# Attention decode on one core: all V tiles in one buffer, the last tiles in pieces, K and V loads in turn, PSUM zeroed by ScalarE and VectorE

## The chip, the cores and the metric

The kernel runs on one core of one Trainium2 chip. A core has a matrix engine (TensorE, PE in the profile), a vector engine (VectorE, DVE), a scalar engine (ScalarE, ACT), GpSimd (POOL), and SyncE (SP), which here does nothing but issue DMAs. Sixteen DMA engines bring data from HBM into SBUF; matrix products land in PSUM. The metric is device microseconds of one execution, lower is better: the median of three runs of the kernel before is 655.73 us (655.61 to 658.28).

## What is computed

One decode step of grouped-query attention. One query token with 32 heads reads a cache of 65,536 keys and values for 8 key/value heads; four query heads share one key/value head. Everything is bf16, the head size is 128.

```python
def reference(q, k, v):          # q: 1 x 32 x 1 x 128, k and v: 1 x 8 x 65536 x 128
    ...
    k = jnp.repeat(k, rep, axis=1)
    v = jnp.repeat(v, rep, axis=1)
    scale = D ** -0.5
    scores = jnp.einsum("bhqd,bhkd->bhqk", q, k) * scale
    p = _softmax(scores, axis=-1)
    return jnp.einsum("bhqk,bhkd->bhqd", p, v)
```

K and V together are 268.4 MB, and each byte is used once.

## The kernel before

**Tiles.** For each of the 8 key/value heads (g = 0 to 7) K and V are cut in two halves of 32,768 keys (b = 0, 1). One such half is a tile: 128 partitions, 256 keys in each, 64 KB in each partition, 8.39 MB in all. There are 32 tiles. They are named here K00, K01 (head 0), K10, K11, up to K71, and V00 to V71. The buffer `io` has room for three tiles: slot 0 for V, slot 1 for K of half 0, slot 2 for K of half 1.

**What happens to a K tile.** VectorE transposes it in place in four instructions of 64 keys a partition (L227). Each of them releases two groups of eight matmuls (L370), which add the scores of the tile to the PSUM tensor `sc`. A tile has eight groups; each group counts up `s_sc` by one. `sc` is four PSUM banks; half b fills banks 2b and 2b+1. The matmuls only ever add (`start=False`), so something must set `sc` to zero before a head begins.

**Softmax of a head.** When both K tiles of a head are scored, VectorE takes the maximum of each bank (L232), then of all (L237); TensorE turns it (L412), VectorE takes the maximum for each query head (L241 to L249), ScalarE computes the exponentials of the four banks and their sums (L252) and then counts up `s_ls`, and VectorE transposes the exponentials into `et`, half a head at a time (L263, `weights`).

**What happens to a V tile.** 64 matmuls (L339) multiply `et` by the tile and add to the PSUM tensor `vacc`, which also must be zero at the start of a head. At the end of a tile `s_vc` goes up by one. After both V tiles of a head VectorE folds `vacc` into `vs` (L272, L275, `collect`), TensorE gathers it (L335), VectorE scales it (L287), and a small DMA writes the head's output.

**TensorE's order.** Its program is one loop over h = 0 to 8. At its head it gathers the output of head h-2 (waits for `s_vs`), sums the exponentials (L352, waits for `s_ls`), and writes zeros with five matmuls of a zero matrix into `sc` and `vacc` (L356). Then, for j = 0 and 1: the scores of K tile (h, j), and then the V tile that is two half-steps behind, which is V(h-1, j). So V tiles are always multiplied behind the scores of the next head's K tile.

**VectorE's order.** For each g: the transposes of K(g,0); the wait for V(g-1,0) to be multiplied; `weights(g-1, 1)`; the transposes of K(g,1) with the bank maxima among them; the fold of `vacc`; the softmax of g; `weights(g, 0)`.

**SyncE's order** is the order of the loads, and a load whose wait is not over holds back all behind it. It is K00, K01, V00, K10, K11, V01 and from then on K and V in turn (K20, V10, K21, V11, ...). K(g,b) waits until the scores of K(g-1,b) are done, and V tile number n waits until all n tiles before it are multiplied (`s_vc`). The end is different: V70 goes into slot 1 in two halves as soon as the scores of K70 are done, and V71 into slot 0, in six pieces of 128, 64, 32, 16, 8 and 8 keys (`CUTS`), once V61 is multiplied.

**The last head's V.** V70 lies in slot 1, and so has code of its own in TensorE's loop: 16 turns of a loop of four matmuls (L390), each of which writes the same 16 PSUM rows; GpSimd passes on the landing of its two halves (`s_un`), and each turn counts up `s_vu`. VectorE's `weights(7, 1)` waits for all 16 turns. V71 is multiplied by L339, except its last 16 keys, which go straight into the output product (L423, `TAIL`).

Of the kernel before, what the change touches and what calls it, by code (L numbers as in the profile page):

```python
# [9 lines left out]
ACT = mybir.ActivationFunctionType  # L10
# [3 lines left out]
P = 128  # L14
D = 128
SL = 256
# [3 lines left out]
WB = 160  # L20
PS = 64
TAIL = 16
UN = 16
CUTS = [0, 128, 192, 224, 240, 248, 256]


# [22 lines left out]
def kernel(  # L49
# [15 lines left out]
    def sb(name, shape, dt):  # L65
        return ctx.enter_context(nc.sbuf_tensor(name, shape, dt))
# [7 lines left out]

    io = sb("io", [P, 3 * SL, D], bf16)
    wz = sb("wz", [P, 4, WB], bf16)
    zero = sb("zero", [P, 512], bf16)
# [24 lines left out]
    pf = ps("pf", [P, 512])  # L102
    pl, fin = pb[0:H, 8:12], pf[0:H, 0:D]

    s_q, s_ka, s_kb, s_st = sem("s_q"), sem("s_ka"), sem("s_kb"), sem("s_st")
    s_v = [sem(f"s_v{i}") for i in range(len(CUTS) - 1)]
    s_u = [sem(f"s_u{i}") for i in range(2)]
    s_un = sem("s_un")
# [6 lines left out]
    s_sc, s_pe, s_vb, s_vc, s_vu = sem("s_sc"), sem("s_pe"), sem("s_vb"), sem("s_vc"), sem("s_vu")  # L115

    sp, act, dve, gp, pe = nc.sync, nc.scalar, nc.vector, nc.gpsimd, nc.tensor
    SP = Queue(nc, sp, None)
# [8 lines left out]
    def load(src, g, b, at, s, lo=0, hi=SL):  # L127
        sp.dma_start(
            out=io[:, at * SL + lo:at * SL + hi, :], in_=rows(src, g, b)[:, lo:hi, :]
        ).then_inc(s, 16)  # L130

    def load_k(g, b):
# [36 lines left out]
    GP.mark(gp.memset(zero[:, :], 0.0))  # L169
    n = GP.mark(gp.memset(ident[:, :], 0.0))  # L170
    GP.after(n)
    p_ident = GP.mark(gp.affine_select(
# [1 line left out]
        pattern=[[-1, P]], channel_multiplier=1,  # L174
    ))
    DV.mark(dve.memset(one[:, :], 1.0))
    dve.memset(ls[:, :], 0.0).then_inc(s_ls, 1)
    dve.memset(vs[:, :], 0.0).then_inc(s_vs, 2)
    DV.wait((s_gp, p_ident))

    DV.mark(dve.tensor_reduce(
# [33 lines left out]
            ).then_inc(s_w, 1)  # L215
    GP.wait((s_sc, 16 * G))
    gp.sem_inc(s_w, 4)
    for i in range(2):
        GP.wait((s_u[i], 16))
        gp.sem_inc(s_un, 128 // UN)  # L220


    def transposes(g, b):
        DV.wait(((s_ka, s_kb)[b], 16 * (g + 1)))
        for t0 in range(0, SL, PS):
            part = io[:, (1 + b) * SL + t0:(1 + b) * SL + t0 + PS, :].rearrange("p t d -> p (t d)")
            dve.transpose(out=part.bitcast(u32), in_=part.bitcast(u32)).then_inc(s_kt, 2)  # L227
            yield
# [10 lines left out]
    def softmax(g):  # L239
        DV.wait((s_pe, 4 * g + 3))  # L240
        n = DV.mark(dve.tensor_reduce(  # L241
            out=m4[:, :], in_=pt[0:1, 0:P].rearrange("o (x h) -> o h x", h=H), axis=AX.X, op=ALU.max
        ))
        DV.after(n)
        dve.tensor_scalar_mul(
            out=nrow[:, :, :], in0=m4[:, None, :].to_broadcast([1, 32, H]), scalar1=-SCALE
        ).then_inc(s_nr, 1)
        DV.wait((s_pe, 4 * g + 4))
        d_nmb = DV.mark(dve.tensor_copy(out=nmb[:, :], in_=pb[:, 0:1]))  # L249
        ACTQ.wait((s_dv, d_nmb))  # L250
        for b in range(4):
            a = act.activation(  # L252
                out=ex[:, b, :], in_=sc[:, 512 * b:512 * b + 512], func=ACT.Exp, bias=nmb[:, :],
                scale=SCALE, accum_out=ls[:, b:b + 1],
            )
            ACTQ.mark(a)
        act.wait_ge(s_ac, ACTQ.n)
        act.sem_inc(s_ls, 1)

    def weights(g, b):  # L260
        for i in range(2):
            DV.wait((s_ac, 4 * g + 2 * b + i + 1))
            dve.transpose(out=et[:, i, :], in_=ex[:, 2 * b + i, :]).then_inc(s_et, 1)  # L263

    def reciprocal(g):
# [2 lines left out]
        DV.after(n)  # L268
        return DV.mark(dve.reciprocal(out=rl[:, :], in_=l4[:, :]))

    def collect():
        n = DV.mark(dve.tensor_scalar_mul(out=vs[:, :], in0=vacc[:, 0, :], scalar1=sely[:, 0:1]))  # L272
        for y in range(1, 4):
            DV.after(n)
            i = dve.scalar_tensor_tensor(  # L275
                out=vs[:, :], in0=vacc[:, y, :], scalar=sely[:, y:y + 1], in1=vs[:, :],
                op0=ALU.mult, op1=ALU.add,
            )
            if y < 3:
                n = DV.mark(i)  # L280
            else:
                i.then_inc(s_vs, 1)

    def finish(g, n_pe, d_rl):
        DV.wait((s_st, 16 * g), (s_pe, n_pe))
# [6 lines left out]
    for g in range(G):  # L292
        for _ in transposes(g, 0):
            pass
        if g:
            DV.wait((s_vc, 2 * g - 1))
# [7 lines left out]
        top()  # L304
        if g:
            d_rl = reciprocal(g - 1)
            DV.wait((s_vc, 2 * g))
            collect()
        softmax(g)
        weights(g, 0)  # L310
        if g:
            finish(g - 1, 4 * g + 5, d_rl)
    DV.wait((s_vu, SL // UN))
    weights(G - 1, 1)
    d_rl = reciprocal(G - 1)
    DV.wait((s_vb, 2 * G - 1))
    collect()
    finish(G - 1, 4 * G + 3, d_rl)
    SP.wait((s_st, 16 * G))

# [25 lines left out]
    with nc.Fori(0, G + 1, 1, engines=OrderedEngineSet([PE]), head_slot={PE: 0}) as h:  # L346
# [3 lines left out]
        gather(start=True, stop=True).then_inc(s_pe, 1)  # L350
        take(s_ls, 1)
        pe.matmul(out=pl, lhsT=sel[:, :], rhs=ls[:, :], start=True, stop=True).then_inc(s_pe, 1)  # L352
        for bank in [sc[:, 512 * b:512 * b + 512] for b in range(4)] + [
            vacc[:, :, :].rearrange("p y d -> p (y d)")
        ]:
            pe.matmul(  # L356
                out=bank, lhsT=zero[:, 0:P], rhs=zero[:, :], start=True, stop=False,
                skip_group_check=True,
            )
        with pe.Fori(0, 2) as j:  # L360
            with pe.If(h < G):
                with pe.Fori(0, 8) as n:
# [18 lines left out]
                    i.then_inc(s_sc, 1)  # L381
            with pe.If(h * 2 + j > 1):
                take(s_et, 2)
                with pe.If(h * 2 + j == 2 * G):
                    with pe.Fori(0, SL // UN) as n:
                        r_v = n * (UN * D) + SL * D
                        r_e = (n // 8) * 512 + (n // 4) % 2 * 16 + (n % 4) * 128
                        take(s_un, 1)
                        for c in range(4):
                            i = pe.matmul(  # L390
                                out=vacc[0:16, :, :],
                                lhsT=bass.AP(et, r_e + c * 32, [[1024, P], [1, 16]]),
                                rhs=bass.AP(io, r_v + c * (4 * D), [[IO, P], [1, 4 * D]]),
                                start=False, stop=False, skip_group_check=True,
                            )
                        i.then_inc(s_vu, 1)
                with pe.Else():
                    for ch in range(4):
                        if ch != 1:
                            take(s_v[max(ch - 1, 0)], 16)  # L400
                        for tt in range(16 if ch < 3 else 12):
                            if (ch, tt) == (3, 8):
                                take(s_v[3], 16)
                            i = wide(ch, tt)
                    i.then_inc(s_vb, 1)
                    with pe.If(h < G):
                        for tt in range(12, 16):
                            i = wide(3, tt)
# [50 lines left out]
```

## Time and profile before

| | |
|---|---|
| median of the runs | 655.73 us |
| the profiled execution, its own time | 658.72 us |
| its span, first to last instruction | 655.3 us |
| PE busy, PE weight loads | 376.2 us, 147.6 us |
| DVE busy | 342.4 us |
| ACT busy, POOL busy | 23.6 us, 7.9 us |
| TensorE clock granted, mean | 0.831 |
| read from HBM | 268.44 MB |

No compute engine is busy for more than 57% of the span. The profile has a row of the rate of the DMAs in 40 slices, a list of DMA issues with the time from issue to landing, and a timeline, whose columns are the start, the duration, engine, line, operation and tensors, the count of merged instructions, and in brackets the idle time before the first of them with what ended it. Where VectorE's transposes (L227) are ended by a DMA, their start tells when a K tile has landed.

### The profile page before, as it was taken

What the parts mean: (1) busy time and instruction counts of PE and PEld (TensorE: products, weight loads), DVE (VectorE), ACT (ScalarE), POOL (GpSimd) and SP (SyncE); (2) the same over time, 40 slices, a digit from 0 to 9 for tenths busy, and PEclk for the clock granted to TensorE, in tenths of its full rate; (3) what the DMA queues carried; (4) which work ended last, traced back from release to release, by engine and by line L of the source; (5) the groups of instructions that cost most, each with busy time, mean ns of one, the idle gap of its engine ahead of it and who ended that gap; (6) DMA issues with size and microseconds to landing.
All of it is one profiled execution on the core that took longest, in us unless ns stands there. A gap on an engine that the chain in (4) does not pass through costs nothing. (4 is left out here: it accounts for less than half of the span.)

```text
span 655.3 us, 7257 instructions
## 1 busy us (share of the span) xinstructions
PE 376.2 (57%) x2167; PEld 147.6 (23%) x2167; DVE 342.4 (52%) x226; ACT 23.6 (4%) x65; POOL 7.9 (1%) x40
## 2 busy tenths in 40 slices
PE   1187466764818656284744838266580866628655
PEld 0032122221303222031311313122130322203212
DVE  1588192936439292564808466193733829156201
ACT  0000100010000100001000010001000010000100
POOL 1000000000000000000000000000000000000000
PEclk9999769795978879597895959879596886959898
DMA  9999991999999999999999999999999999999970
GB/s 382 448 448 400 436 444 68 448 448 413 420 448 444 440 396 448 444 444 392 448 448 444 424 412 448 444 444 392 445 448 444 416 420 448 448 436 396 443 330 0
DMA packets 5589, 268.50 MB, mean 410 GB/s; under 512 B 720, under 2 KB 720, under 8 KB 1104
## 3 DMA queue, kind: packets, MB, share of 16 engines
q1 hardware_dynamic: 5480, 268.44, 94.9%
q10 hardware_dynamic: 104, 0.02, 0.0%
q14 instruction: 4, 0.03, 0.0%
q8 instruction: 1, 0.02, 0.0%
HBM read 268.44 MB, written 0.01 MB: 410 GB/s over the span
## 5 line engine op out<-in xcount | busy, mean ns | idle before, releaser
L370 PE MATMUL sc<-io,wz 128*128 x1024 | 272.5, 418 | 217.0 <-PEq L325 174.6
L227 DVE STREAM_TRANSPOSE io<-io 128x4096 uint32<-128x4096 uint32 x64 | 279.5, 4415 | 109.4 <-DMA io<-in_k_dram 109.4
L370 PEld LDWEIGHTS sc<-io,wz 128*128 x1024 | 106.0, 104 | 386.8 <-issue 308.6
L263 DVE STREAM_TRANSPOSE et<-ex 128x512 bf16<-128x512 bf16 x32 | 21.5, 701 | 117.3 <-PE vacc L339 81.3
L339 PE MATMUL vacc<-io,et 128*16 128x512 bf16 x956 | 55.7, 387 | 5.3 <-PEq L325 5.3
L232 DVE TENSOR_REDUCE mx<-sc 128x1 f32<-128x512 f32 x32 | 20.8, 668 | 49.7 <-PE sc L370 49.7
L252 ACT ACTIVATE ex<-sc,nmb 128x512 bf16<-128x512 f32 x32 | 21.6, 685 | 589.8 <-DVE nmb L249 589.8
L339 PEld LDWEIGHTS vacc<-io,et 128*16 128x16 bf16 x956 | 24.6, 91 | 36.3 <-issue 14.1
L390 PE MATMUL vacc<-io,et 128*16 x64 | 16.7, 384 | 9.6 <-PEq L325 9.6
L356 PE MATMUL sc<-zero 128*128 128x512 bf16 x36 | 17.0, 628 | 0.0
L272 DVE TENSOR_SCALAR vs<-vacc,sely 128x128 f32<-128x128 f32 x8 | 2.8, 350 | 24.6 <-PE vacc L339 24.6
L352 PE MATMUL pb<-ls,sel 128*4 128x4 f32 x18 | 1.8, 169 | 19.1 <-PEq L325 19.1
L212 POOL COPY wz<-qT 32x16 bf16<-32x16 bf16 x32 | 6.1, 191 | 520.0 <-PE sc L370 516.7
L414 PE MATMUL pb<-one,nrow 1*128 1x1 f32 x16 | 2.8, 241 | 14.3 <-PEq L325 14.3
L390 PEld LDWEIGHTS vacc<-io,et 128*16 x64 | 5.5, 86 | 21.2 <-issue 17.9
L335 PE MATMUL pf<-vs,sel 128*4 128x128 f32 x20 | 4.2, 295 | 9.9 <-PEq L325 9.2
L275 DVE SCALAR_TENSOR_TENSOR vs<-vacc,sely,vs 128x128 f32<-128x128 f32 x24 | 8.4, 351 | 0.9
L252 ACT ACTIVATION_READ_ACCUMULATOR ex<-sc,nmb 128x1 f32 x32 | 6.5, 202 | 0.0
L352 PEld LDWEIGHTS pb<-ls,sel 128*4 128x4 f32 x18 | 1.2, 86 | 21.6 <-issue 21.4
L414 PEld LDWEIGHTS pb<-one,nrow 1*128 1x128 f32 x16 | 2.3, 182 | 15.6 <-issue 15.6
L356 PE MATMUL vacc<-zero 128*128 128x512 bf16 x9 | 5.7, 634 | 0.0
L356 PEld LDWEIGHTS sc<-zero 128*128 128x128 bf16 x36 | 3.9, 131 | 5.3 <-issue 5.0
(29 smaller groups left out, 23.9 us busy)
## 6 DMA issues: line engine op xcount, KB each, us to landing
io<-in_v_dram SPq DMA_DIRECT2D x3, 4096.0 KB, 38.0
io<-in_v_dram SPq DMA_DIRECT2D x1, 2048.0 KB, 23.6
io<-in_v_dram SPq DMA_DIRECT2D x1, 1024.0 KB, 25.7
io<-in_v_dram SPq DMA_DIRECT2D x1, 512.0 KB, 26.4
io<-in_v_dram SPq DMA_DIRECT2D x2, 256.0 KB, 26.7
io<-in_k_dram SPq DMA_DIRECT2D x16, 47.7
io<-in_v_dram SPq DMA_DIRECT2D x14, 28.9
out_dram<-o ACTq DMA_DIRECT2D x7, 1.0 KB
```

The costliest lines, as they stand in the source:

```text
L212: gp.tensor_copy(out=wz[r, :, c0:c0 + H].rearrange("p (s w) h -> p s w h", s=2), in_=qTb[r, :, :, g, :],).then_inc(s_w, 1)
L227: dve.transpose(out=part.bitcast(u32), in_=part.bitcast(u32)).then_inc(s_kt, 2)
L232: return DV.mark(dve.tensor_reduce(out=mx[:, b:b + 1], in_=sc[:, 512 * b:512 * b + 512], axis=AX.X, op=ALU.max))
L252: a = act.activation(out=ex[:, b, :], in_=sc[:, 512 * b:512 * b + 512], func=ACT.Exp, bias=nmb[:, :], scale=SCALE, accum_out=ls[:, b:b + 1],)
L263: dve.transpose(out=et[:, i, :], in_=ex[:, 2 * b + i, :]).then_inc(s_et, 1)
L275: i = dve.scalar_tensor_tensor(out=vs[:, :], in0=vacc[:, y, :], scalar=sely[:, y:y + 1], in1=vs[:, :], op0=ALU.mult, op1=ALU.add,)
L335: return pe.matmul(out=fin, lhsT=sel[:, :], rhs=vs[:, :], skip_group_check=True, **kw)
L339: return pe.matmul(out=vacc[32 * c:32 * c + 16, :, :], lhsT=et[:, ch // 2, w0:w0 + 16], rhs=io[:, PS * ch + 4 * tt:PS * ch + 4 * tt + 4, : ...
L356: pe.matmul(out=bank, lhsT=zero[:, 0:P], rhs=zero[:, :], start=True, stop=False, skip_group_check=True,)
L370: i = pe.matmul(out=bass.AP(sc, r_o, [[2048, P], [1, 512]]), lhsT=bass.AP(wz, r_w + ((2 * s + e) * WB - 4 * u), [[4 * WB, P], [1, P]]), rh ...
L390: i = pe.matmul(out=vacc[0:16, :, :], lhsT=bass.AP(et, r_e + c * 32, [[1024, P], [1, 16]]), rhs=bass.AP(io, r_v + c * (4 * D), [[IO, P], [ ...
L414: pe.matmul(out=pb[:, 0:1], lhsT=nrow[:, :, :].rearrange("o x h -> o (x h)"), rhs=one[:, :], start=True, stop=True,).then_inc(s_pe, 1)
```

## The change

- **Loads of K.** K00 is loaded in two halves and K71 in four quarters, each piece with a semaphore of its own, and VectorE waits for the piece that it transposes.
- **Order of the loads.** After K00 and K01 it is K and V in turn from the start: K10, V00, K11, V01, K20, V10, ...
- **Loads of V.** All 16 V tiles go into slot 0. A V tile now counts up `s_vc` twice, once at half and once at the end. V61 and V70 are loaded in halves, each half as soon as the same half of the tile before is multiplied. Of V71 the first 128 keys wait for the first half of V70, and the other five pieces for its second half.
- **TensorE.** The loop for V70 (L390), `s_un`, `s_vu` and GpSimd's part in them are gone; V70 takes the same 64 matmuls as every other V tile. The five matmuls that write zeros (L356) are gone.
- **Zeros.** `sc` is set to zero by one ScalarE instruction of 128 x 2048 after the exponentials of each head but the last, ahead of the count of `s_ls`; `vacc` by one VectorE memset of 128 x 512 at the end of `collect`, ahead of the count of `s_vs`. For head 0 five VectorE memsets do both.
- **VectorE's order.** `softmax(g)` stands ahead of the reciprocal and `collect` of the head before; both come ahead of `weights(g, 0)` as before.

The core of the diff:

```diff
+    k_cuts = {(0, 0): [0, 128, 256], (G - 1, 1): [0, 64, 128, 192, 256]}
...
     def load_k(g, b):
         SP.wait((s_sc, 16 * g - 8 + 8 * b if g else 0))
-        load(k, g, b, 1 + b, (s_ka, s_kb)[b])
+        cuts = k_cuts.get((g, b), [0, SL])
+        for lo, hi in zip(cuts, cuts[1:]):
+            k_ready[g, b, lo] = key = s_k[b, lo], k_count.get((b, lo), 0) + 16
+            k_count[b, lo] = key[1]
+            load(k, g, b, 1 + b, key[0], lo, hi)
 
     def load_v(g, b):
-        if g < G - 1:
-            SP.wait((s_vc, 2 * g + b))
+        done = 2 * (2 * g + b)
+        if (g, b) == (G - 1, 1):
+            SP.wait((s_vc, done - 1))
+            load(v, g, b, 0, s_v[0], CUTS[0], CUTS[1])
+            SP.wait((s_vc, done))
+            for lo, hi, s in list(zip(CUTS, CUTS[1:], s_v))[1:]:
+                load(v, g, b, 0, s, lo, hi)
+        elif (g, b) in ((G - 2, 1), (G - 1, 0)):
+            for i in range(2):
+                SP.wait((s_vc, done - 1 + i))
+                load(v, g, b, 0, s_v[i], 128 * i, 128 * i + 128)
+            for s in s_v[2:4]:
+                sp.sem_inc(s, 16)
+        else:
+            SP.wait((s_vc, done))
             load(v, g, b, 0, s_v[0])
             for s in s_v[1:4]:
                 sp.sem_inc(s, 16)
-        elif b == 0:
-
-            SP.wait((s_sc, 16 * g + 8))
-            for i in range(2):
-                load(v, g, b, 1, s_u[i], 128 * i, 128 * i + 128)
-        else:
-            SP.wait((s_vc, 2 * g))
-            for lo, hi, s in zip(CUTS, CUTS[1:], s_v):
-                load(v, g, b, 0, s, lo, hi)
...
     load_k(0, 1)
-    load_v(0, 0)
-    load_k(1, 0)
-    load_k(1, 1)
-    load_v(0, 1)
-    for g in range(2, G):
+    for g in range(1, G):
         for b in range(2):
             load_k(g, b)
             load_v(g - 1, b)
...
+    for b in range(4):
+        DV.mark(dve.memset(sc[:, 512 * b:512 * b + 512], 0.0))
+    n = DV.mark(dve.memset(vacc[:, :, :], 0.0))
...
             ACTQ.mark(a)
+        n = ACTQ.n
+        if g == 0:
+            ACTQ.wait((s_dv, d_zero))
+        if g < G - 1:
+            ACTQ.after(n)
+            ACTQ.mark(act.activation(
+                out=sc[:, :], in_=zero[:, 0:1].to_broadcast([P, 4 * 512]), func=ACT.Copy
+            ))
         act.wait_ge(s_ac, ACTQ.n)
         act.sem_inc(s_ls, 1)
...
+        if not last:
+            DV.after(n)
+            n = DV.mark(dve.memset(vacc[:, :, :], 0.0))
+        DV.after(n)
+        dve.sem_inc(s_vs, 1)
...
-                with pe.If(h * 2 + j == 2 * G):
-                    with pe.Fori(0, SL // UN) as n:
...
+                    if ch == 1:
                         i.then_inc(s_vc, 1)
+                i.then_inc(s_vb, 1)
+                with pe.If(h * 2 + j < 2 * G + 1):
+                    for tt in range(12, 16):
+                        i = wide(3, tt)
+                    i.then_inc(s_vc, 1)
```

**Where rows move.** Each fence below holds the program's rows of one engine in their order: line, operation, tensor written and read, shape, and the semaphores that a row waits for.

On SyncE, the first loads before (`in_k_dram` and `in_v_dram` are K and V in HBM; 128x32768 elements are a whole tile):

```order
L128 DMA io<-in_k_dram 128x32768 x2
L128 DMA io<-in_v_dram 128x32768
L128 DMA io<-in_k_dram 128x32768 [waits s_sc] x2
L128 DMA io<-in_v_dram 128x32768 [waits s_vc]
L128 DMA io<-in_k_dram 128x32768 [waits s_sc]
```

and the same place now:

```order
L125 DMA io<-in_k_dram 128x16384 x2
L125 DMA io<-in_k_dram 128x32768
L125 DMA io<-in_k_dram 128x32768 [waits s_sc]
L125 DMA io<-in_v_dram 128x32768
L125 DMA io<-in_k_dram 128x32768 [waits s_sc]
L125 DMA io<-in_v_dram 128x32768 [waits s_vc]
```

V00, which was third in the queue and waited for nothing, is now behind K10 and so behind the scores of K00; V01, which was behind K11 as well, keeps its place as the sixth tile and its wait for V00 to be multiplied.

On SyncE, the last loads before, from V60 on (K71 is ahead of V61, the third row; V70 is the two rows of 128x16384 behind it):

```order
L128 DMA io<-in_v_dram 128x32768 [waits s_vc]
L128 DMA io<-in_k_dram 128x32768 [waits s_sc]
L128 DMA io<-in_v_dram 128x32768 [waits s_vc]
L128 DMA io<-in_v_dram 128x16384 [waits s_sc]
L128 DMA io<-in_v_dram 128x16384
L128 DMA io<-in_v_dram 128x16384 [waits s_vc]
L128 DMA io<-in_v_dram 128x8192
L128 DMA io<-in_v_dram 128x4096
L128 DMA io<-in_v_dram 128x2048
L128 DMA io<-in_v_dram 128x1024 x2
```

and now, again from V60 on:

```order
L125 DMA io<-in_v_dram 128x32768 [waits s_vc]
L125 DMA io<-in_k_dram 128x8192 [waits s_sc]
L125 DMA io<-in_k_dram 128x8192 x3
L125 DMA io<-in_v_dram 128x16384 [waits s_vc] x5
L125 DMA io<-in_v_dram 128x8192 [waits s_vc]
L125 DMA io<-in_v_dram 128x4096
L125 DMA io<-in_v_dram 128x2048
L125 DMA io<-in_v_dram 128x1024 x2
```

K71 is in quarters, V61 and V70 in halves, and V70 no longer waits for scores but, half by half, for V61 to be multiplied, as V71 does for V70.

On VectorE, between the maximum of all banks and the transposes of the next K tile, in the middle of the run, before:

```order
L237 TENSOR_REDUCE mg<-mx 128x1 [waits s_dv]
L267 TENSOR_REDUCE l<-pb 4x1 [waits s_pe]
L269 RECIPROCAL rl<-l 4x1 [waits s_dv]
L272 TENSOR_SCALAR vs<-vacc,sely 128x128 [waits s_vc]
L275 SCALAR_TENSOR_TENSOR vs<-vacc,sely,vs 128x128 [waits s_dv] x3
L241 TENSOR_REDUCE m<-pt 1x4 [waits s_pe]
L245 TENSOR_SCALAR nrow<-m 1x128 [waits s_dv]
L249 COPY nmb<-pb 128x1 [waits s_pe]
L263 STREAM_TRANSPOSE et<-ex 128x512 [waits s_ac] x2
```

and now:

```order
L247 TENSOR_REDUCE mg<-mx 128x1 [waits s_dv]
L251 TENSOR_REDUCE m<-pt 1x4 [waits s_pe]
L255 TENSOR_SCALAR nrow<-m 1x128 [waits s_dv]
L259 COPY nmb<-pb 128x1 [waits s_pe]
L285 TENSOR_REDUCE l<-pb 4x1 [waits s_pe]
L287 RECIPROCAL rl<-l 4x1 [waits s_dv]
L290 TENSOR_SCALAR vs<-vacc,sely 128x128 [waits s_vc]
L293 SCALAR_TENSOR_TENSOR vs<-vacc,sely,vs 128x128 [waits s_dv] x3
L300 MEMSET vacc 128x512 [waits s_dv]
L281 STREAM_TRANSPOSE et<-ex 128x512 [waits s_dv,s_ac]
```

The softmax rows moved ahead of the six rows of the head before, and the memset of `vacc` stands between them and the transposes into `et`.

More of the change, by code (lines that the diff above doesn't have):

```diff
@@ L76 @@
     wz = sb("wz", [P, 4, WB], bf16)
-    zero = sb("zero", [P, 512], bf16)
+    zero = sb("zero", [P, 1], fp32)
     ident = sb("ident", [P, P], fp32)
@@ L176 @@
     DV.mark(dve.memset(one[:, :], 1.0))
-    dve.memset(ls[:, :], 0.0).then_inc(s_ls, 1)
-    dve.memset(vs[:, :], 0.0).then_inc(s_vs, 2)
+    n = DV.mark(dve.memset(ls[:, :], 0.0))
+    d_zero = DV.mark(dve.memset(zero[:, :], 0.0))
+    DV.mark(dve.memset(vs[:, :], 0.0))
+    for b in range(4):
+        DV.mark(dve.memset(sc[:, 512 * b:512 * b + 512], 0.0))
+    n = DV.mark(dve.memset(vacc[:, :, :], 0.0))
+    DV.after(n)
+    dve.sem_inc(s_ls, 1)
+    dve.sem_inc(s_vs, 2)
     DV.wait((s_gp, p_ident))
@@ L217 @@
     gp.sem_inc(s_w, 4)
-    for i in range(2):
-        GP.wait((s_u[i], 16))
-        gp.sem_inc(s_un, 128 // UN)
     def transposes(g, b):
-        DV.wait(((s_ka, s_kb)[b], 16 * (g + 1)))
         for t0 in range(0, SL, PS):
+            if (g, b, t0) in k_ready:
+                DV.wait(k_ready[g, b, t0])
             part = io[:, (1 + b) * SL + t0:(1 + b) * SL + t0 + PS, :].rearrange("p t d -> p (t d)")
@@ L269, in reciprocal, with collect @@
         return DV.mark(dve.reciprocal(out=rl[:, :], in_=l4[:, :]))
-    def collect():
+    def collect(last=False):
         n = DV.mark(dve.tensor_scalar_mul(out=vs[:, :], in0=vacc[:, 0, :], scalar1=sely[:, 0:1]))
@@ L295 @@
         if g:
-            DV.wait((s_vc, 2 * g - 1))
+            DV.wait((s_vc, 4 * g - 2))
             weights(g - 1, 1)
@@ L312 @@
             finish(g - 1, 4 * g + 5, d_rl)
-    DV.wait((s_vu, SL // UN))
+    DV.wait((s_vc, 4 * G - 2))
     weights(G - 1, 1)
     d_rl = reciprocal(G - 1)
-    DV.wait((s_vb, 2 * G - 1))
-    collect()
+    DV.wait((s_vb, 2 * G))
+    collect(last=True)
     finish(G - 1, 4 * G + 3, d_rl)
@@ L352 @@
         pe.matmul(out=pl, lhsT=sel[:, :], rhs=ls[:, :], start=True, stop=True).then_inc(s_pe, 1)
[L353 to L359, printed above, removed]
         with pe.Fori(0, 2) as j:
@@ L383 @@
                 take(s_et, 2)
-                with pe.If(h * 2 + j == 2 * G):
-                    with pe.Fori(0, SL // UN) as n:
[L386 to L408, printed above, removed]
-                        i.then_inc(s_vc, 1)
+                for ch in range(4):
+                    if ch != 1:
+                        take(s_v[max(ch - 1, 0)], 16)
+                    for tt in range(16 if ch < 3 else 12):
+                        if (ch, tt) == (3, 8):
+                            take(s_v[3], 16)
+                        i = wide(ch, tt)
+                    if ch == 1:
+                        i.then_inc(s_vc, 1)
+                i.then_inc(s_vb, 1)
[3 more added lines that the diff above has]
+                    i.then_inc(s_vc, 1)
         with pe.If(h < G):
```

23 lines of the change are left out of this document (10 added, 13 removed).

## The prediction

> **What bounds the kernel now.** First the page: its span, its rows of DMA busy share and rate in 40 slices, the load queue, and from its list of DMA issues the last two pieces of V71 (count, size, us from issue to landing).
>
> ```profile
> span 655.3 us, 7257 instructions
> ...
> DMA  9999991999999999999999999999999999999970
> GB/s 382 448 448 400 436 444 68 448 448 413 420 448 444 440 396 448 444 444 392 448 448 444 424 412 448 444 444 392 445 448 444 416 420 448 448 436 396 443 330 0
> ...
> q1 hardware_dynamic: 5480, 268.44, 94.9%
> ...
> io<-in_v_dram SPq DMA_DIRECT2D x2, 256.0 KB, 26.7
> ```
>
> The loads keep the DMA engines at nine tenths or more in every slice but three: the seventh, and the last two. So the stream of loads is the bound, and what can be won lies in the hole near 100 us and in the time after the stream. The timeline of the first 160 us, then the rate in two stretches (the last figures are DMA share and GB/s), then the time to landing of V01, issued at 111.32:
>
> ```profile
> 24.25 17.42 DVE L227 STREAM_TRANSPOSE io<-io 128x4096 uint32<-128x4096 uint32 x4 [19.69 <-DMA io<-in_k_dram]
> 29.72 7.56 PE L370 MATMUL sc<-io,wz 128*128 x24 [21.00 <-PEq L325]
> ...
> 43.59 8.77 DVE L227 STREAM_TRANSPOSE io<-io 128x4096 uint32<-128x4096 uint32 x2 [1.92 <-DMA io<-in_k_dram]
> ...
> 49.59 21.54 SPq L128 DMA_DIRECT2D io<-in_k_dram  x2
> ...
> 68.85 1.92 PE L370 MATMUL sc<-io,wz 128*128 x8 [0.61 <-issue]
> ...
> 74.21 1.38 DVE L263 STREAM_TRANSPOSE et<-ex 128x512 bf16<-128x512 bf16 x2 [0.85 <-ACT ex L252]
> ...
> 75.98 0.21 ACT L252 ACTIVATION_READ_ACCUMULATOR ex<-sc,nmb 128x1 f32 x1
> ...
> 82.32 17.42 DVE L227 STREAM_TRANSPOSE io<-io 128x4096 uint32<-128x4096 uint32 x4 [6.72 <-DMA io<-in_k_dram]
> ...
> 111.32 0.33 SPq L128 DMA_DIRECT2D io<-in_v_dram  x1
> ...
> 153.50 17.43 DVE L227 STREAM_TRANSPOSE io<-io 128x4096 uint32<-128x4096 uint32 x4 [6.91 <-DMA io<-in_k_dram]
> ```
>
> ```profile
> 98.00:102.00 4.00, 3.35 (x16) 1.43 (x15) 1.74 (x1) 0.00 (x0) 0.00 (x0) 1.00 0.04 16
> ...
> 106.00:110.00 4.00, 3.73 (x51) 1.62 (x53) 0.00 (x0) 0.00 (x0) 0.00 (x0) 1.00 0.00 0
> ```
>
> ```profile
> io<-in_v_dram SPq DMA_DIRECT2D x1, 21.8
> ```
>
> K00 is there at 24.25 and K01 at 43.59: **one tile takes 19.34 us** in the stream. Into an empty queue it takes 21.8 us from issue to landing, 2.5 more. K20 is the seventh tile; in an unbroken stream it would come at 24.25 + 6 x 19.34 = 140.3, and it came at 153.50. The hole costs 13.2 us: V01 waits until V00 is multiplied, and that waits for the scores of K10, whose transposes began at 82.32. **From a K tile's first transpose to the next V issue it is 29.0 us** (82.32 to 111.32).
>
> From the timeline of a later head:
>
> ```profile
> 226.85 0.19 PE L352 MATMUL pb<-ls,sel 128*4 128x4 f32 x2 [2.42 <-PEq L325]
> ...
> 230.92 17.42 DVE L227 STREAM_TRANSPOSE io<-io 128x4096 uint32<-128x4096 uint32 x4 [4.63 <-DMA io<-in_k_dram]
> 236.35 4.93 PE L370 MATMUL sc<-io,wz 128*128 x16 [7.06 <-PEq L325]
> ...
> 256.26 3.63 PE L339 MATMUL vacc<-io,et 128*16 128x512 bf16 x64 [0.23 <-PEq L325]
> 259.93 0.33 SPq L128 DMA_DIRECT2D io<-in_v_dram  x1
> ```
>
> Scores start 5.4 us after the first transpose and take 19.7 (236.35 to 256.03); V takes 3.63. The V issue at 259.93 comes 9.7 us before the K tile in flight lands (230.92 + 2 x 19.34 = 269.6): here the stream never stops, and nothing that the change does to the engines costs time while it stays below such margins.
>
> The end, on the timeline; then the times to landing of V61 (issued at 570.60) and of the first two pieces of V71 (the first issued at 609.25):
>
> ```profile
> 541.53 17.42 DVE L227 STREAM_TRANSPOSE io<-io 128x4096 uint32<-128x4096 uint32 x4 [4.66 <-DMA io<-in_k_dram]
> ...
> 580.22 8.77 DVE L227 STREAM_TRANSPOSE io<-io 128x4096 uint32<-128x4096 uint32 x2 [8.31 <-DMA io<-in_k_dram]
> ...
> 617.27 2.35 PE L390 MATMUL vacc<-io,et 128*16 x8
> ...
> 643.63 1.31 DVE L263 STREAM_TRANSPOSE et<-ex 128x512 bf16<-128x512 bf16 x2 [29.29 <-PE vacc L390]
> ...
> 645.50 4.92 PE L339 MATMUL vacc<-io,et 128*16 128x512 bf16 x60 [1.91 <-PEq L325]
> ...
> 650.47 0.35 DVE L272 TENSOR_SCALAR vs<-vacc,sely 128x128 f32<-128x128 f32 x1 [5.32 <-PE vacc L339]
> ...
> 652.04 0.38 PE L335 MATMUL pf<-vs,sel 128*4 128x128 f32 x2 [0.73 <-DVE vs L275]
> ...
> 652.88 0.35 SPq L290 DMA_DIRECT2D out_dram<-o  x1
> ```
>
> ```profile
> 570.60 1.36 SPq L128 DMA_DIRECT2D io<-in_v_dram  x3
> ...
> 609.25 2.96 SPq L128 DMA_DIRECT2D io<-in_v_dram  x6
> ```
>
> ```profile
> io<-in_v_dram SPq DMA_DIRECT2D x1, 28.9
> ...
> io<-in_v_dram SPq DMA_DIRECT2D x1, 4096.0 KB, 19.4
> io<-in_v_dram SPq DMA_DIRECT2D x1, 2048.0 KB, 23.6
> ```
>
> The last piece is issued at 609.25 + 2.96 - 0.33 = 611.9 and lands 26.7 later, at 638.5. The stream is over then, yet the span ends at 655.3, 16.8 us later: V70 is multiplied from 617.27 to 643.6 in its own slow loop, and V71, long there, waits for it.
>
> **The change, part by part.**
>
> *The start.* Half of K00 comes at 24.25 - 9.67 = 14.6, its scores start at 20.0 and end, by 19.7, at 39.7; the second half, at 24.25, is just in time for its groups (29.7 against 29.9). So K10 is issued at about 39.7 instead of 49.59, 3.9 us before K01 lands, and V00 with it: no hole there. Scores of K01 start at 43.59 + 5.4 = 49.0, since TensorE is free, and end at 68.7. From the end of the scores (70.77) to the end of the transposes into `et` (75.59) it was 4.8 us, so K10, landed long before, is transposed from 73.5 on, and V01 is issued at 73.5 + 29.0 = 102.5. The stream runs out at 24.25 + 4 x 19.34 = 101.6. From the issue of V01 to K20 it was 42.2 us (111.32 to 153.50), so K20 comes at 144.7: **8.8 us saved**, and 4.4 of the 13.2 remain.
>
> *Zeros.* Their nearest rows, from the groups by line and from the timeline of VectorE's first instructions:
>
> ```profile
> L252 ACT ACTIVATE ex<-sc,nmb 128x512 bf16<-128x512 f32 x32 | 21.6, 685 | 589.8 <-DVE nmb L249 589.8
> ...
> L232 DVE TENSOR_REDUCE mx<-sc 128x1 f32<-128x512 f32 x32 | 20.8, 668 | 49.7 <-PE sc L370 49.7
> ```
>
> ```profile
> 1.11 0.17 DVE L178 MEMSET vs<- 128x128 f32 x1
> ```
>
> The ScalarE instruction writes four times the elements of L252: between 0.69 us and 4 x 0.685 = 2.74; I take 2.3, nearer the upper end, since the elements go one by one. It delays `s_ls`. In the later heads L352 stood ready at 226.85 for scores at 236.35, 9.5 us of cover (the five zero matmuls that filled part of it go, at no gain). In head 0 the cover is thinner: exponentials end at 76.19 - 2.0 = 74.1, zeros at 76.4, scores of K10 are due at 73.5 + 5.4 = 78.9: 2.5 us to spare, nothing at the upper end either. A memset of `vacc` lies between 0.17 and 0.67; I take 0.6. With the fold (1.5 us) it now delays the `et` transposes, under the 4.63 us in which VectorE waited for K30; the five at the start lie in its 19.69 us wait, of which 10 remain. Cost of all: nothing.
>
> *V61 and V70 at the end.* I count from K70's first transpose (541.53 before) as L. V61 is issued at L + 29.1, `et` follows 1.3 later, and only then are the quarters of K71 transposed: L + 30.4 (the whole tile came at L + 38.7). Scores start at L + 35.8 and end at L + 55.5; half of V61 takes 0.2 + 1.8, so the first half of V70 is issued at L + 57.5. V61 lands at 570.60 + 28.9 = L + 58.0, so the queue is all but empty: by the 2.5 us that an issue into an empty queue costs, V70's half lands at L + 69.7 and not at L + 67.7. **2.0 us lost.** Behind it there is cover: its second half is issued at L + 60; `weights(7, 0)` is ready near L + 66; V71 follows each half of V70 with 7 us to spare. The Trainium skill (DMA: Bandwidth & Descriptors, Anatomy of one DMA — SWDGE (gpsimd) path) gives about 2.0 us of fixed cost for a DMA that GpSimd issues, where this trace has 2.5 for SyncE's; by it the loss would be 1.5.
>
> *The end.* After the last piece: `collect` (650.47 to 651.98, 1.5 us) starts when all but the last 16 keys are multiplied, two pieces before the last, so it ends about 0.8 us after the landing; from the gather to the end it is 652.04 to 655.3, 3.3 us; 0.2 for a TensorE that waits between pieces. So 4.3 us instead of 16.8: **12.5 us saved**.
>
> *Sum.* 8.8 + 12.5 - 2.0 = 19.3 us. The profiled execution has a span of 655.3 and a time of 658.72, the median is 655.73; the same saving brings the span to 636.0, that execution's time to 639.4 and the median to **636.4 us**.
>
> **The rivals.**
>
> *The halves of K00 gain nothing* (they land together, or SyncE is late). K10 is then issued at 49.6 into an empty queue, lands at 71.4, is transposed from 75.6; the stream then has V01 in time, and K20 comes at 71.4 + 4 x 19.34 = 148.8: 4.1 us later, **640.5**. For it: margin 3.9 - 2.5 us only. Against: the first two V71 pieces land 4.8 us apart, in order.
>
> *The quarters of K71 gain nothing.* Scores end at L + 63.8, V70's first half is issued at L + 65.8 and is 10.2 late: **644.6**.
>
> *The stream never stops*, as issues overlap more than I count: the remaining 4.4 and 2.0 go, **630.0**.
>
> *The end stays with the engines*: V70 and V71 still trail the stream, and the 12.5 stay: **648.9**. Against it: the block of 64 matmuls takes 3.63 us in every other head, not 26.
>
> *Slower: loads in pieces run below the stream's rate.* K00, K71 and V61 are newly cut, 25.2 MB or 58.0 us. To eat 19.3 us they must run at three quarters of the rate or less; at half the rate the time would be 636.4 + 58.0 = **694**. Against it: V71's second piece, 16 KB in each partition as in the quarters of K71, landed at about 609.75 + 23.6 = 633.4, the first at 628.7: 2.1 MB in 4.7 us, the stream's own rate. [...]
>
> **How the numbers follow.** Forecast 0.62; halves 0.12; quarters 0.06; never stops 0.11; engines 0.05; pieces slow 0.02; the rest spread. The range reaches down to near 630 and up over the halves' 640.5 with the bounds of the tail (4 to 5.5 us): 630.5 to 642.5. 0.5% is 3.3 us, about what a measurement of this kernel can tell from no change; only the slow pieces and mishaps reach it: faster 0.96, same 0.02, slower 0.02.
>
> **What would show it.** K10 issued near 40 and V01 near 102.5; K20's transposes from about 144.7; then a K tile every 19.34 us; V70's first half issued about when V61 lands; the last landing near 632 and about 4 us to the end. It is wrong if the DMA row shows a new hole in a slice that is full now, if the scores of K10 wait for the ScalarE zeros, or if pieces land slower than the stream.

## The result and the profile after

The changed kernel takes **637.8 us** (median of four runs, 637.22 to 638.14) against 655.67 us before; the ratio is 0.9718, with a 95% interval of 0.9692 to 0.9745. The forecast was 636.4, in a range of 630.5 to 642.5.

The page of the changed kernel: span, DMA busy share and rate in 40 slices, the load queue, two groups of instructions that are new, and the time to landing of the last two pieces of V71.

```profile
span 635.4 us, 7032 instructions
...
DMA  8999998999999999999999999999999999999896
GB/s 367 456 392 433 425 446 347 437 458 400 458 400 462 421 437 458 400 458 400 462 417 441 458 401 458 400 458 408 450 454 404 462 396 462 396 432 429 367 432 259
...
q1 hardware_dynamic: 6200, 268.44, 98.1%
...
L272 ACT ACTIVATE sc<-zero 128x2048 f32<-128x2048 f32 x7 | 13.2, 1880 | 0.3
...
L300 DVE MEMSET vacc<- 128x512 f32 x7 | 3.4, 485 | 1.3 <-DVE vs L293 1.3
...
io<-in_v_dram SPq DMA_DIRECT2D x2, 256.0 KB, 14.0
```

The seventh slice, which had a busy share of one tenth before, has eight; the last slice, which had none, has six. The queue's share went from 94.9% to 98.1% of a shorter span.

The timeline of the first 150 us of the changed kernel:

```profile
0.96 39.14 SPq L125 DMA_DIRECT2D io<-in_k_dram  x4
...
40.14 0.43 SPq L125 DMA_DIRECT2D io<-in_v_dram  x1
...
73.51 17.38 DVE L237 STREAM_TRANSPOSE io<-io 128x4096 uint32<-128x4096 uint32 x4
...
76.35 0.19 PE L372 MATMUL pb<-ls,sel 128*4 128x4 f32 x2 [4.40 <-PEq L345]
78.89 9.50 PE L383 MATMUL sc<-io,wz 128*128 x32 [2.35 <-PEq L345]
...
102.12 0.33 SPq L125 DMA_DIRECT2D io<-in_v_dram  x1
...
144.04 8.77 DVE L237 STREAM_TRANSPOSE io<-io 128x4096 uint32<-128x4096 uint32 x2 [6.67 <-DMA io<-in_k_dram]
```

K10 is the last of the four loads merged in the first row, issued at 0.96 + 39.14 - 0.33 = 39.77; V00 follows at 40.14, where before it was third in the queue. K10 is transposed from 73.51, V01 issued at 102.12, and K20 comes at 144.04, where it came at 153.50: **9.5 us saved** at the start.

The end of the changed kernel's timeline: first the instructions, then the issues of the last five pieces of V71, then two stretches with TensorE's granted clock (the third column from the right), and last the time to landing of the first half of V70, issued at 588.82:

```profile
532.04 17.43 DVE L237 STREAM_TRANSPOSE io<-io 128x4096 uint32<-128x4096 uint32 x4 [4.66 <-DMA io<-in_k_dram]
...
561.92 8.73 DVE L237 STREAM_TRANSPOSE io<-io 128x4096 uint32<-128x4096 uint32 x2
...
586.87 1.90 PE L359 MATMUL vacc<-io,et 128*16 128x512 bf16 x32
...
630.20 1.86 PE L425 MATMUL pf<-io,et 128*4 128x128 bf16 x16 [0.43 <-issue]
...
631.86 0.63 PE L355 MATMUL pf<-vs,sel 128*4 128x128 f32 x2
...
632.96 0.35 SPq L310 DMA_DIRECT2D out_dram<-o  x1
```

```profile
614.42 2.29 SPq L125 DMA_DIRECT2D io<-in_v_dram  x5
```

```profile
628.00:630.00 2.00, 1.52 (x12) 0.50 0.79 301
630.00:632.00 2.00, 1.80 (x17) 0.50 0.00 0
```

```profile
io<-in_v_dram SPq DMA_DIRECT2D x1, 4096.0 KB, 12.1
```

The last of the five pieces in the row at 614.42 is issued at 616.3 and lands 14.0 later, at 630.3. From there to the end it is 5.1 us, where it was 16.8: **11.7 us saved**. From K70's first transpose to the last landing it was 638.5 - 541.5 = 97.0 us and is 630.3 - 532.0 = 98.3: **1.3 us lost**. Between K20 and K70 nothing changed (541.53 - 153.50 = 388.0 us, 532.04 - 144.04 = 388.0). 9.5 + 11.7 - 1.3 = 19.9, which is the difference of the two spans, 655.3 - 635.4.

The medians differ by 17.9 us and not by 19.9: the spans of the kernel before lie between 652.8 and 655.7 us, most of them under 654.5, and the profiled one was among the longer, as the last experiment below shows.

### The profile page after: what moved, and what is told of

The parts are those of the page before. It is cut to its first block, busy times and chain, and to the rows that moved or that the text cites. A ratio compares the mean times of both kernels' runs of the same rounds, so it can differ in the third digit from the quotient of the medians.

```text
span 635.4 us, 7032 instructions
## 1 busy us (share of the span) xinstructions
PE 351.1 (55%) x2122; PEld 139.9 (22%) x2122; DVE 347.4 (55%) x239; ACT 36.7 (6%) x72; POOL 7.4 (1%) x39
## 3 DMA queue, kind: packets, MB, share of 16 engines
q1 hardware_dynamic: 6200, 268.44, 98.1%
## 5 line engine op out<-in xcount | busy, mean ns | idle before, releaser
L359 PE MATMUL vacc<-io,et 128*16 128x512 bf16 x1020 | 65.3, 409 | 20.1 <-PEq L345 20.1
L359 PEld LDWEIGHTS vacc<-io,et 128*16 128x16 bf16 x1020 | 26.5, 93 | 57.8 <-issue 36.7
L251 DVE TENSOR_REDUCE m<-pt 1x4 f32<-1x128 f32 x8 | 2.2, 278 | 22.7 <-PE pt L413 22.7
L272 ACT ACTIVATE sc<-zero 128x2048 f32<-128x2048 f32 x7 | 13.2, 1880 | 0.3
L355 PEld LDWEIGHTS pf<-vs,sel 128*4 128x4 f32 x20 | 1.3, 87 | 27.2 <-issue 27.2
L300 DVE MEMSET vacc<- 128x512 f32 x7 | 3.4, 485 | 1.3 <-DVE vs L293 1.3
L259 DVE COPY nmb<-pb 128x1 f32<-128x1 f32 x8 | 1.3, 158 | 4.3 <-PE pb L415 4.3
```

The lines of the kernel that those rows point to most:

```text
L272: ACTQ.mark(act.activation(out=sc[:, :], in_=zero[:, 0:1].to_broadcast([P, 4 * 512]), func=ACT.Copy))
L300: n = DV.mark(dve.memset(vacc[:, :, :], 0.0))
L355: return pe.matmul(out=fin, lhsT=sel[:, :], rhs=vs[:, :], skip_group_check=True, **kw)
L359: return pe.matmul(out=vacc[32 * c:32 * c + 16, :, :], lhsT=et[:, ch // 2, w0:w0 + 16], rhs=io[:, PS * ch + 4 * tt:PS * ch + 4 * tt + 4, : ...
```

## The experiments

Spans below are those of profiled executions, to be set against 635.4 us of the changed kernel. The four executions of the changed kernel have spans of 635.4 to 636.3 us, so where a kernel ran once, differences under about 1 us mean nothing; the kernels with K01 or K70 in halves and those behind them ran four times or more, all others here once.

### Each half of the saving by itself

First the changed kernel with the old first loads:

```diff
-    k_cuts = {(0, 0): [0, 128, 256], (G - 1, 1): [0, 64, 128, 192, 256]}
+    k_cuts = {(G - 1, 1): [0, 64, 128, 192, 256]}
...
     load_k(0, 1)
-    for g in range(1, G):
+    load_v(0, 0)
+    load_k(1, 0)
+    load_k(1, 1)
+    load_v(0, 1)
+    for g in range(2, G):
```

> The changed kernel with the old first loads (K00 whole, V00 third, then K10, K11, V01); the rest stays changed. Theory (the start saved the wait for V00 behind a late K10): the hole comes back, K20's first transpose at about 153.5 instead of 144.0, span 635.4 + 9.5 = 644.9. Rival (the order of the loads is indifferent, the end saved it all): 635.4.

Then the kernel before with the new first loads alone:

```diff
...
+        if (g, b) == (0, 0):
+            load(k, g, b, 1, s_k0, 0, 128)
+            load(k, g, b, 1, s_ka, 128, 256)
+        else:
+            load(k, g, b, 1 + b, (s_ka, s_kb)[b])
...
-    load_v(0, 0)
-    load_k(1, 0)
-    load_k(1, 1)
-    load_v(0, 1)
-    for g in range(2, G):
+    for g in range(1, G):
...
```

> The kernel before with the new first loads alone (K00 in halves, K and V in turn from the start); the end, V70's own loop and the zeros stay as before. Theory: K20's first transpose near 144, everything behind it 9.5 us earlier, V70's loop still ends last, 16.8 us from the last landing to the end: span 655.3 - 9.5 = 645.8. Rival (the slow end takes up what the start gains): 655.

Measured: spans of 644.0 and 645.9 us, where 644.9 and 645.8 were expected. The timeline of the second, at K20 and at the end:

```profile
145.12 17.42 DVE L233 STREAM_TRANSPOSE io<-io 128x4096 uint32<-128x4096 uint32 x4 [6.67 <-DMA io<-in_k_dram]
```

```profile
635.70 1.31 DVE L269 STREAM_TRANSPOSE et<-ex 128x512 bf16<-128x512 bf16 x2 [29.29 <-PE vacc L396]
...
643.44 0.35 SPq L296 DMA_DIRECT2D out_dram<-o  x1
```

VectorE still waits 29.29 us at the end for V70's own loop (L396 here), the same as before; it only does so earlier. K20 comes 153.50 - 145.12 = 8.4 us earlier. By the spans the start is thus worth 8.6 us with the new end and 9.4 with the old one, but the second is set against the long execution of 655.3; the kernel before ran beside these runs with a span of 653.7. By whole times the start alone saves 655.67 - 648.02 = 7.7 us and the end alone 655.67 - 645.86 = 9.8, together 17.5 of the 17.9. Neither part takes up what the other gains. Within the end, only the quarters of K71 are taken away by themselves below; the halves of V61 and V70, the new place of V70 and VectorE's new order are not.

### The halves of K00, the quarters of K71

```diff
-    k_cuts = {(0, 0): [0, 128, 256], (G - 1, 1): [0, 64, 128, 192, 256]}
+    k_cuts = {(G - 1, 1): [0, 64, 128, 192, 256]}
```

> The changed kernel with K00 in one piece. Theory: K00 scored at 49.6 instead of 39.7, K10 issued then into an empty queue and landed near 71.4, K20's first transpose at 148.8 instead of 144.0: span 635.4 + 4.8 = 640.2. Rival (the halves gain nothing, the order alone did it): 635.4.

```diff
-    k_cuts = {(0, 0): [0, 128, 256], (G - 1, 1): [0, 64, 128, 192, 256]}
+    k_cuts = {(0, 0): [0, 128, 256]}
```

> The changed kernel with K71 in one piece. Theory: K71's transposes start when all of it has landed, 8.8 us later, the first half of V70 is issued 8.8 us later into a queue that has run empty: span 635.4 + 8.8 = 644.2. Rival (quarters gain nothing, the queue has cover): 635.4.

Measured: 640.6 us (642.38 in all) with K00 whole, 645.0 (646.77) with K71 whole. With K00 whole, the first loads and K20:

```profile
0.96 48.64 SPq L125 DMA_DIRECT2D io<-in_k_dram  x3
49.64 0.43 SPq L125 DMA_DIRECT2D io<-in_v_dram  x1
```

```profile
149.28 17.42 DVE L237 STREAM_TRANSPOSE io<-io 128x4096 uint32<-128x4096 uint32 x4 [5.25 <-DMA io<-in_k_dram]
```

K10 is issued at 0.96 + 48.64 - 0.33 = 49.3, after K01 has landed, and K20 comes 5.2 us later than with halves. With K71 whole its transposes start 9.05 us later (570.97 against 561.92; K70's start stands at 532.26):

```profile
570.97 8.77 DVE L237 STREAM_TRANSPOSE io<-io 128x4096 uint32<-128x4096 uint32 x2 [8.76 <-DMA io<-in_k_dram]
```

and the span is 9.6 us longer. The expectations were 640.2 and 644.2. Both tiles in pieces are needed for the saving: each lets the next issue come before the queue has run empty.

### The zeros

The changed kernel with zeros from TensorE again:

```diff
...
-        if g < G - 1:
-            ACTQ.after(n)
-            ACTQ.mark(act.activation(
-                out=sc[:, :], in_=zero[:, 0:1].to_broadcast([P, 4 * 512]), func=ACT.Copy
-            ))
...
+        for bank in [sc[:, 512 * b:512 * b + 512] for b in range(4)] + [
+            vacc[:, :, :].rearrange("p y d -> p (y d)")
+        ]:
+            pe.matmul(
+                out=bank, lhsT=zero[:, 0:P], rhs=zero[:, :], start=True, stop=False,
+                skip_group_check=True,
+            )
```

> The changed kernel with the zeros written by TensorE's five matmuls again, and no zeroing by ScalarE or VectorE. Theory (the zeros were under cover before and are now): span 635.4, within 0.5. Rival (the five matmuls stood in the path of each head, 2.5 us): 635.4 + 8 x 2.5 = 655.

The changed kernel with ScalarE's zeroing three times:

```diff
-            ACTQ.after(n)
-            ACTQ.mark(act.activation(
-                out=sc[:, :], in_=zero[:, 0:1].to_broadcast([P, 4 * 512]), func=ACT.Copy
-            ))
+            for _ in range(3):
+                ACTQ.after(n)
+                n = ACTQ.mark(act.activation(
+                    out=sc[:, :], in_=zero[:, 0:1].to_broadcast([P, 4 * 512]), func=ACT.Copy
+                ))
...
```

> The changed kernel with the ScalarE zeroing done three times in each head (two more of 1.9 us each). Theory (cover of 2.4 us in head 0, over 9 us in the later heads): the scores of K10 start about 1.5 us later, and so does all behind: span 636.9. Rival (every head pays): 635.4 + 7 x 3.8 = 662.

Measured: 635.8 us with TensorE's zeros, so that part of the change is worth nothing that one run can tell, as forecast. Three times the zeroing: 639.0 us, 3.6 more and not 1.5. Its timeline at head 0:

```profile
80.48 0.19 PE L373 MATMUL pb<-ls,sel 128*4 128x4 f32 x2 [8.22 <-PEq L346]
82.00 9.63 PE L384 MATMUL sc<-io,wz 128*128 x32 [1.32 <-PEq L346]
```

```profile
147.24 4.45 DVE L237 STREAM_TRANSPOSE io<-io 128x4096 uint32<-128x4096 uint32 x1 [6.77 <-DMA io<-in_k_dram]
```

The mechanism is the expected one, in head 0 alone: scores of K10 start 3.1 us later (82.00 against 78.89), K20 3.2 us later, and the later heads add next to nothing. But the cover was smaller than reckoned: after the sums (L373) another 1.32 us pass on TensorE's sequencer before the first scores, though the data was there: K10's transposes began at 73.82, and in the changed kernel the scores followed 5.4 us behind (78.89 - 73.51), which here would be 79.2. So of the 2.35 us of idle time in the changed kernel's row of 78.89 only about 1.0 was cover.

### What is left in the stream

```diff
-    k_cuts = {(0, 0): [0, 128, 256], (G - 1, 1): [0, 64, 128, 192, 256]}
+    k_cuts = {(0, 0): [0, 128, 256], (0, 1): [0, 128, 256], (G - 1, 1): [0, 64, 128, 192, 256]}
```

> The changed kernel with K01 in halves too. Theory (what is left of the hole hangs on the scores of K01): scores of K01 start as soon as those of K00 end and end near 59.5, V01 is issued near 93, well before the stream runs out at 101.6, K20's first transpose at 140.3: span 635.4 - 3.7 = 631.7. Rival (the hole has another cause): 635.4.

```diff
-    k_cuts = {(0, 0): [0, 128, 256], (G - 1, 1): [0, 64, 128, 192, 256]}
+    k_cuts = {(0, 0): [0, 128, 256], (G - 1, 0): [0, 128, 256], (G - 1, 1): [0, 64, 128, 192, 256]}
```

> The changed kernel with K70 in halves too. Theory (the first half of V70 was 1.0 to 1.3 us late because K71's transposes wait for V60, and V60 for K70): K70's transposes start up to 4.6 us earlier, the first half of V70 is issued near 584, ahead of V61's landing: span 635.4 - 1.1 = 634.3. Rival (that loss is the price of small pieces): 635.4.

Measured: 632.9 us with K01 in halves and 634.0 us with K70 in halves; medians of four runs 634.19 us (ratio to the kernel before 0.9662, 0.9634 to 0.9690) and 636.47 us (0.9701, 0.9674 to 0.9729). With K70 in halves the first half of V70 is issued at 584.41, 4.4 us earlier, lands 16.0 us later, at 600.4, in the unbroken stream, and the loss of about 1 us is gone. That this profiled execution is 1.4 us shorter, where 1.1 was expected, is in part luck: 0.9 us of it comes from TensorE's clock at the end (see below), while its start was 0.4 us later. With K01 in halves K20's first transpose stands here:

```profile
141.57 17.42 DVE L237 STREAM_TRANSPOSE io<-io 128x4096 uint32<-128x4096 uint32 x4 [4.63 <-DMA io<-in_k_dram]
```

That is 2.5 us saved and not the 3.7 expected. The time to landing of K10, issued at 39.8 in this kernel, and then of K10 in the next kernel, which has K00 in quarters as well and issues it at 34.73:

```profile
io<-in_k_dram SPq DMA_DIRECT2D x1, 24.3
```

```profile
io<-in_k_dram SPq DMA_DIRECT2D x1, 28.2
```

39.8 + 24.3 = 64.1, and 34.73 + 28.2 = 62.9, which is the unbroken stream's time (24.25 + 2 x 19.34). So an issue about 4 us ahead of the landing of the tile before was still 0.8 us late here (K01 landed at 43.9, and 43.9 + 19.34 = 63.3), and one 9 us ahead was not. The loss at such a lead varies: in the seven traces where K10 is issued 3.8 to 4.3 us ahead it is 0.1 to 1.3 us, while of the 31 loads in all traces that were issued 5.4 to 6.5 us ahead one lost 0.6 us and none of the others more than 0.1. That next kernel has all three tiles in more pieces:

```diff
-    k_cuts = {(0, 0): [0, 128, 256], (G - 1, 1): [0, 64, 128, 192, 256]}
+    k_cuts = {
+        (0, 0): [0, 64, 128, 192, 256], (0, 1): [0, 128, 256],
+        (G - 1, 0): [0, 128, 256], (G - 1, 1): [0, 64, 128, 192, 256],
+    }
...
```

> The changed kernel with K00 in quarters, K01 in halves and K70 in halves. Theory (both losses left in the stream are late issues): K10 is issued near 35 and follows K01 without the 0.9 us that it lost after halves, V01 is in time, K20's first transpose at about 140.7 instead of 144.0, the first half of V70 is in time: span 635.4 - 3.3 - 1.0 = 631.1, and 630.2 where TensorE's clock is up in the last microseconds. Rival (small pieces cost what the earlier start saves): 633 or more.

```profile
140.39 17.42 DVE L240 STREAM_TRANSPOSE io<-io 128x4096 uint32<-128x4096 uint32 x4 [4.63 <-DMA io<-in_k_dram]
```

Measured: span 630.4 us (expected 631.1), median of six runs 632.36 us, ratio to the kernel before 0.9649 (0.9606 to 0.9692). One of the six took 640.45 us, with a mean granted clock of 0.616 against 0.80 to 0.81 in the other five; it stands in the ratio and widens its interval, and no trace of it was taken. K20 comes at 140.39; the unbroken stream gives 140.3.

### The last five microseconds

The same kernel with matmuls that compute nothing wanted while TensorE waits for the pieces of V71: 12 and 3 in the first, 14, 4 and 4 in the second, shown here:

```diff
                 for ch in range(4):
+                    if ch in (0, 2, 3):
+                        with pe.If(h * 2 + j == 2 * G + 1):
+                            for _ in range((14, 0, 4, 4)[ch]):
+                                pe.matmul(
+                                    out=pt[:, :], lhsT=wz[:, 0, 0:P], rhs=et[:, 1, :],
+                                    start=True, stop=True, skip_group_check=True,
+                                )
```

> The same with 12 and 3 further matmuls of 512 columns into an unused bank while TensorE waits for pieces of V71. Theory (the last landing to the end takes 5.1 us instead of 4.3 because TensorE runs at half its clock there): clock above 0.9 from about 4 us into the wait on, last landing to end 4.2 to 4.3 us, span 630.2. Rival (the order of VectorE's fold sets the end, not the clock): last landing to end stays at 5.1, as in the kernel without them.

> The kernel with K00 in quarters, K01 and K70 in halves, and 14, 4 and 4 further matmuls of 512 columns into an unused bank ahead of the first 64 keys, the third 64 and the last 64 of V71. Theory (TensorE's clock, not the order of the work, makes the time from the last landing to the end 5.1 us instead of 4.2): with the pauses between 620 and 624 us filled too the clock stays above 0.9 to the end, the last 16 matmuls take about 1.05 us instead of 1.86, last landing to end is 4.2 to 4.3 us, span 629.6. Rival (the end is set by something else): the clock is up, and last landing to end stays at 5.1, span 630.5.

Measured: 630.6 us (median 632.54, ratio 0.9627, 0.9602 to 0.9653) and 629.9 us (median 631.78, ratio to the kernel before 0.9621, 0.9595 to 0.9647). In the first the clock was up at 616 to 620 us and back at half from 622 on, so its theory of the clock failed and it tells nothing of the question. The clock of the second by stretches, and its end:

```profile
620.00:624.00 4.00, 2.62 (x28) 1.00 0.78 307
624.00:626.00 2.00, 1.09 (x17) 0.99 0.05 17
626.00:628.00 2.00, 1.03 (x9) 0.50 0.00 0
```

```profile
625.30 1.31 PE L435 MATMUL pf<-io,et 128*4 128x128 bf16 x16 [0.67 <-DMA io<-in_v_dram]
626.40 0.64 PE L358 MATMUL pf<-vs,sel 128*4 128x128 f32 x2
...
627.50 0.35 SPq L313 DMA_DIRECT2D out_dram<-o  x1
```

The clock is up until 626 and half again behind it: the 16 last matmuls take 1.31 us instead of 1.86, the gather still 0.64, and from the last landing (625.4) to the end it is 4.5 us. The 4.2 to 4.3 us expected were thus reached only in part. In the kernel with K70 in halves the clock happened to be up without help, and the same stretch was 4.2 us:

```profile
630.00:632.00 2.00, 1.10 (x16) 1.00 0.00 0
```

```profile
629.69 1.05 PE L425 MATMUL pf<-io,et 128*4 128x128 bf16 x16 [0.64 <-DMA io<-in_v_dram]
630.72 0.38 PE L355 MATMUL pf<-vs,sel 128*4 128x128 f32 x2
```

So the clock makes most of the difference between 5.1 and 4.2 us. When it changes can be read from the traces: in all fourteen, every stretch between two changes is a whole multiple of 3.41 us. By the matmuls' busy time in the step of 3.41 us before, the clock rose behind 2.64 us or more and stayed at half behind up to 2.74; it fell behind up to 1.80 us and stayed up behind 1.41 or more. With K70 in halves the step from 624.94 to 628.36 happened to hold 2.80 us of matmuls, in the changed kernel the one from 626.10 to 629.51 only 2.56; with the longer filling the step from 622.54 to 625.95 held 1.65, and the clock fell.

The kernel with all the pieces and the longer filling, at 631.78 us, is the fastest of all that ran.

### The kernel before, once more

> The kernel before, unchanged, profiled once more. Its first profiled execution took 658.72 us against a median of 655.7, and 3.4 us lay around its span, against 1.8 for every other kernel here. Theory (that execution was a slow one, so that the spans show 2 us more saving than the medians): span near 653.8 with 1.9 us around it. Rival (this kernel always has more around its span): span 652.3 with 3.4 around it, or 655.3 again.

Measured: the profiled execution took 658.38 us with a span of 655.1, again one of the longer. Of its ten executions four had spans of 654.8 to 655.5 us with about 3.1 around them, and six of 652.8 to 654.0 with 2.1 around them; the median was 656.1. So the expectation for the profile (653.8) failed. The profile came out as the rival's second figure (655.3 again, with 3.3 around it), but not for the rival's reason, since the time around the span is not fixed: the executions of this kernel differ by up to 3.6 us, and both profiles caught long ones. Where the shorter ones save their 1 to 2 us of span is open, since no trace of one was taken.

## Why the prediction was right

- **What bounds it.** The stream of loads, a hole at the start and a slow end: confirmed by taking each part alone, 7.7 us for the start and 9.8 for the end by whole times.
- **The start** was sized at 8.8 us and measured 9.5. K10's issue (39.77 against 39.7), its first transpose (73.51 against 73.5) and V01's issue (102.12 against 102.5) came as worked out. "No hole there" behind K01 was not quite right: K10 came 0.9 us late, though issued 3.9 us ahead. The remaining hole was thus made of two late issues, not one, as K01 in halves (2.5 us) and K00 in quarters (the rest) showed.
- **The zeros** cost nothing, as forecast: ScalarE's took 1.88 us (estimate 2.3), the memset of `vacc` 0.49 (estimate 0.6). The cover in head 0 was put at 2.5 us and is about 1.0, because the time from the sums to the first scores was left out.
- **V70's first half** was to be 2.0 us late and was 0.9; the end of the stream lost 1.3 in all, 0.2 of it in the quarters of K71. Issued at 588.82, 1.5 us ahead of V61's landing at 590.3, it landed 12.1 us later, where half a tile takes 9.7 in the unbroken stream. The 2.4 us more are near the 2.5 of the forecast. The seven loads that were issued into an empty queue, over all the traces, took 2.4 to 3.2 us more than in the stream. The Trainium skill (DMA: Bandwidth & Descriptors, Anatomy of one DMA — SWDGE (gpsimd) path) has about 2.0 us of fixed cost for a DMA that GpSimd issues. These traces, for SyncE's DMAs, have more. The size was off because the issue came at L + 56.8 and not at L + 57.5 (588.82 - 532.04), most of it since K71's transposes started at L + 29.9 instead of L + 30.4, and because V61 landed at L + 58.3 instead of L + 58.0.
- **The end** was to take 4.3 us from the last landing and took 5.1: the 0.2 us allowed for a TensorE that waits between pieces should have been about 1.0. The granted clock was 0.50 in the last stretches, and the forecast had left it out. The Trainium skill (TensorE: Matmul & The Clock Gate, Part 1: The HAM clock gate) says that the clock falls to half after an idle window of about 3.4 us and rises after a busy one. The traces agree on the length, 3.41 us, but the window before a fall need not be idle: with the longer filling TensorE was busy for 1.65 us of it.
- **The sum** was 19.3 us; the spans differ by 19.9. Some of that closeness is luck: the start saved 0.7 us more than forecast, the stretch from K70 to the last landing lost 0.7 less, and the end saved 0.8 less. Carried over to the medians the sum gave 636.4, and 637.8 was measured: the profiled execution that served as the base was one of the longer ones, so the kernel had less to lose than its profile showed.
- **The rivals.** With K00 whole the kernel took 4.6 us more in all (forecast 4.1), with K71 whole 9.0 (forecast 8.2). The stream did stop, so 630.0 was not reached: the changed kernel lost 0.9 us at K10, 2.6 at V01 and 0.9 at V70's first half. The end did not stay with V70: 5.1 us from the last landing, not 16.8. Pieces did not run slower than whole tiles: halves land 9.7 us apart, and the four quarters of K71 together take 19.6 us against 19.34. The forecast's own row for this was read slightly wrong: the second piece of V71 was issued at 609.99 and not at about 609.75, so the two pieces landed 4.9 us apart and not 4.7, which is still the stream's rate (a quarter of 19.34 is 4.8).

## What to carry to other kernels

Where a stream of loads is the bound, look for the few places where it stands still, and follow each one back to the wait that issues the next load; loading the tile at the head of that chain in pieces moves the whole chain by the time of the missing pieces. An issue has to come well ahead of the end of the queue: here a lead of about 4 us still lost 0.1 to 1.3 us, one of 5.4 us or more almost never anything, and a queue that had run empty cost 2.4 to 3.2 us on top. Before a saving is subtracted from a median, see whether the profiled execution is a typical one.

## What the runs showed of the hardware

- From the sums at the head of TensorE's loop to the first matmul of the scores 1.32 us pass on its sequencer, with the data there (the row at 82.00 in the run with three zeroings).
- A ScalarE copy of 128 x 2048 fp32 zeros into four PSUM banks takes 1.88 us, less than three times the 0.69 us of an exponential of 128 x 512; a VectorE memset of one bank takes 0.49 us.
- In the last microseconds TensorE ran at half its clock in the changed kernel: 16 matmuls of 128 columns took 1.86 us there and 1.05 with the clock up.
- In all these traces TensorE's clock changed only at steps of 3.41 us: it rose behind steps with at least 2.64 us of matmuls, and once up it held behind some with as little as 1.41.
